# A fused spectral and expert kernel: five output tiles instead of four, and a build-time plan that counts them

## The chip, the cores and the metric

The kernel runs on one core of a Trainium2 chip, where nothing else runs. The metric is the device time of one execution in microseconds (us). The kernel before took 427.27 us (median of 3 runs, 426.96 to 428.14). One execution of each kernel was also recorded by the profiler, and the traces shown here are of those. In them DVE is VectorE, ACT ScalarE, PE TensorE's matmuls, PEld its weight loads, POOL GpSimd, SP SyncE; L with a number is a line of that kernel's source, so the same statement has different numbers in different kernels.

## The reference, cut to what matters

```python
# x: (8, 2496, 256) float32
X = rfft(x, axis=1);  Y = softshrink(X @ (w_r + i w_i) + (b_r + i b_i), 0.01)
y = irfft(Y, axis=1)                                  # (8, 2496, 256)
e = argmax(mean(y, axis=1) @ w_gate)                  # one of 8 experts per batch row
out = softmax_gate * (relu(y @ w1[e]) @ w2[e])        # w1[e] 256x1024, w2[e] 1024x256
```

The kernel does the transforms as matmuls in fp16 and works on two batch rows at a time: while one row ("batch" below) is in its expert stage, the next is in its transforms. Batches are counted from 0; those with a transposition are 1 to 6. A batch in the steady part takes some 50 us.

## The kernel before

The order of instructions on every engine comes from a list scheduler in the kernel itself. It runs when the kernel is built and takes, one after the other, the piece of work that can start soonest by its own estimates. A `Tok` stands for a buffer of a ring; a piece that needs one can't be planned before the piece that frees the owner of that place.

```python
    def ready(self, o):
        ...
        for k in o.allocs:
            if k.tag in self.rings: ...
            else:
                h = self.hist.setdefault(k.tag, [])
                prev = h[-k.bufs : len(h) - k.bufs + 1] if len(h) >= k.bufs else []
            for p in prev:
                for r in p.rel:
                    if r.done is None:
                        return None
                    t = max(t, r.done)
        return t
```

Output tiles (`ost`, 128 x 512 float32) come from a pool of four. A result is evicted (copied out of the memory that matmuls write to) into such a tile, and the tile is stored to DRAM. The plan doesn't count these tiles. On the chip the fifth request waits until the store of the first has landed.

```python
    BUFS = {"XT": 2, "hs": 2, "z": 3, "V": 3, "Pt": 2}
    opool = pool("op", 4)
    ...
    # add_turned: last 192 columns of a batch; evicted, transposed 32x32 on VectorE, stored in four pieces
        def ev(eng):
            oc["o"] = ost = opool.tile([P, 2, D], FP32, name="ost")     # tile 10 of the batch
            ...
        e = S.evac(2 * n, ev, v, deps=[m, gb_op])
        def tr(_):
            oc["t"] = ot = opool.tile([P, 2, D], FP32, name="ost")      # tile 11 of the batch
            nc.vector.transpose(out=ot..., in_=oc["o"]...)
        e = S.op("DVE", 0.5, tr, v, deps=[e], lat=0.6)
        ...
        S.op("POOL", 3.0, st, v, deps=[e], dma=1.2)
    ...
    # transforms of the next batch, group q: the sum that a complex product by three matmuls needs
            def sm(_, cell=cell):                                       # L895
                X = cell["X"].rearrange("p h a r i k -> p (h a) r (i k)")
                nc.vector.tensor_add(out=X[:, :, 2], in0=X[:, :, 0], in1=X[:, :, 1])
            so = S.op("DVE", 0.34, sm, vt(f + 0.01), deps=e_ops, lat=0.48)
            ...                                                         # L914: matmuls that read X
```

Of the kernel before, what the change touches and what calls it, by code (L numbers as in the profile page):

```python
# [113 lines left out]
class Ring:  # L114
# [13 lines left out]
    def take(self, k):  # L128
        p = self.first(k)
        for i in range(p, p + k.wide):  # L130
            self.owner[i] = k
        self.at = (p + k.wide) % len(self.owner)
        return p
# [115 lines left out]
def kernel(  # L249
# [21 lines left out]
    def pool(name, bufs, **kw):  # L271
        return ctx.enter_context(tc.tile_pool(name=name, bufs=bufs, **kw))
# [2 lines left out]
    XIN = 5 * XROW + 2 * D  # L275
    XF = 2
    X0_CUTS = ((4, 12), (12, 20), (20, 22))
    BUFS = {"XT": 2, "hs": 2, "z": 3, "V": 3, "Pt": 2}
    cpool = pool("consts", 1)
    xpool = pool("xp", 2)  # L280
    apool = pool("ap", 1)
    bpool = pool("bp", 2)
    ppool = pool("pp", BUFS["Pt"])
    tpool = pool("tp", BUFS["XT"])
    zpool = pool("zp", BUFS["z"])
    Ypool = pool("Yp", BUFS["z"])
    vpool = pool("vp", BUFS["V"])
    v2pool = pool("v2p", 2)
    ypool = pool("yp", 2)
    hpool = pool("hp", BUFS["hs"])  # L290
    wpool = pool("wp", 2)
    gpool = pool("gp", 2)
    opool = pool("op", 4)
    spool = pool("sp", 1)
    dpool = pool("dp", 2, space=bass.MemoryType.DRAM)
    psum = pool("ps", 1, space=bass.MemoryType.PSUM)
# [88 lines left out]
    S = Schedule(BANKS)  # L385
# [14 lines left out]
    def bank(tag):  # L400
        return ps[:, BASE[tag] + S.bank[tag]]
# [53 lines left out]
    for i in range(WARM):  # L455
        def dummy(_):
            nc.tensor.matmul(pw, warm[:, 0:P], warm)
        o = S.op("PE", 0.43 if i < COLD else 0.216, dummy, 1e6 + i)
# [18 lines left out]
    c1, c2, c3 = ([S.fixed(t)] for t in X0_AT[1:])  # L477
# [736 lines left out]
    def add_fast(b, c, ns, nl, cell, h_ops, hk, wk, tt, gb_op, v0):  # L1214
        (t0, t1_, t2, t3), t_tok = tt
        th, m = nl // 2, nl // 4
# [4 lines left out]
        vt = lambda x: v0 + PERIOD * (c * 8 + 8 + x) / 44  # L1221
# [36 lines left out]
        def prod(x, dst, a, bb, start, deps, allocs=(), after=None):  # L1258
            def mm(_):
                if start:  # L1260
                    fc[dst[0]] = bank(tag).rearrange(
                        "p (h i c) -> p h i c", h=2, i=2)
                for t in range(2):
                    for f in range(4):
                        nc.tensor.matmul(  # L1265
                            fc[dst[0]][0:m, dst[1], t, :], A[a](f, t), bb(f),
                            start=start and t == 0 and f == 0,
                            stop=f == 3,
                            skip_group_check=True)
            return S.mm([P] * 8, mm, vt(x), deps=deps, allocs=allocs, after=after)  # L1270

        ost = lambda t, h: fc["o", t][0:m, :, P * h : P * h + P]

        def take(x, t, h, deps):
            def ev(eng):
                if ("o", t) not in fc:
                    fc["o", t] = opool.tile([P, 2, D], FP32, name="ost")
                src = fc["E"][0:m, 0]
                if eng == "ACT":
                    nc.scalar.activation(out=ost(t, h), in_=src, func=AFT.Copy,  # L1280
                                         scale=gbc_t[b][0:m])
                else:
                    nc.vector.tensor_scalar_mul(out=ost(t, h), in0=src,
                                                scalar1=gbc_t[b][0:m])
            return S.evac(256, ev, vt(x), deps=deps)

        def add(x, t, h, half, deps):
            def ad(_):
                nc.vector.scalar_tensor_tensor(  # L1289
                    out=ost(t, h), in0=fc["F"][0:m, half], scalar=gbc_t[b][0:m],  # L1290
                    in1=ost(t, h), op0=ALU.mult, op1=ALU.add)
            return S.op("DVE", 0.36, ad, vt(x), deps=deps, lat=0.5)

        p1 = prod(0, ("E", 0), "11", w2(0, 0), True, h_ops[:4], [ek])
        c1 = take(0.1, 0, 0, [p1, gb_op])
        p2 = prod(1.2, ("F", 0), "12", w2(1, 0), True, h_ops, [fk], p1)
        p5 = prod(2.4, ("F", 1), "S1", T(0), False, [o1, t0], after=p2)
        a11 = add(2.5, 0, 0, 0, [p5, c1])
        p6 = prod(3.6, ("E", 0), "S2", T(1), False, [o2, c1, t1_], after=p5)
        u2 = take(3.7, 0, 1, [p6])  # L1300
        p7 = prod(4.8, ("E", 0), "S3", T(2), False, [o3, u2, t2], after=p6)
        u3 = take(4.9, 1, 1, [p7])
        a22 = add(5.0, 1, 1, 1, [u3, p5, a11])
        p4 = prod(6.0, ("E", 0), "22", T(3), False, [u3, t3], after=p7)
        c21 = take(6.1, 1, 0, [p4])
# [8 lines left out]
        for t, deps in ((0, [a11, a12]), (1, [c21, a22])):  # L1314
            def st(_, t=t):
                nc.sync.dma_start(
                    out=out[b, ns + th * t : ns + th * t + th, :].rearrange(
                        "(p i) c -> p i c", i=2),
                    in_=fc["o", t][0:m])
            S.op("SP", 0.3, st, vt(8), deps=deps, dma=0.75)  # L1320

    T_t = {}

    def add_turned(b, ns, nl, s0, cell, h_ops, hk, wk, gb_op, v):

        n = nl - s0
        tag = "o"
        ok = S.tok(tag, BANKS[tag])
        oc = {}
        for h in range(2):  # L1330
            def mm(_, h=h):
                if h == 0:
                    oc["p"] = bank(tag)[:, 0 : 2 * n].rearrange(
                        "p (h t) -> p h t", h=2)
                for ft in range(E):
                    nc.tensor.matmul(  # L1336
                        oc["p"][:, h],
                        w2s_t[b][:, ft].rearrange("p (m h) -> p h m", h=2)[:, h],
                        cell["hs"][:, ft, s0:nl],
                        start=(ft == 0), stop=(ft == E - 1))  # L1340
            m = S.mm([n] * E, mm, v, deps=h_ops, after=m if h else None,
                     allocs=[] if h else [ok])
            hk.rel.append(m)
            wk.rel.append(m)

        def ev(eng):
            oc["o"] = ost = opool.tile([P, 2, D], FP32, name="ost")
            o = ost.rearrange("p h c -> p (h c)")[:, 0 : 2 * n].rearrange(
                "p (h t) -> p h t", h=2)
            if eng == "ACT":  # L1350
                nc.scalar.activation(out=o, in_=oc["p"], func=AFT.Copy,
                                     scale=gbc_t[b])
            else:
                nc.vector.tensor_scalar_mul(out=o, in0=oc["p"],
                                            scalar1=gbc_t[b])
        e = S.evac(2 * n, ev, v, deps=[m, gb_op])
        ok.rel.append(e)

        def tr(_):
            oc["t"] = ot = opool.tile([P, 2, D], FP32, name="ost")  # L1360
            nc.vector.transpose(
                out=ot.rearrange("p h c -> p (h c)")[:, 0 : 2 * n].rearrange(
                    "p (t c h) -> p h t c", h=2, c=32),
                in_=oc["o"].rearrange("p h c -> p (h c)")[:, 0 : 2 * n].rearrange(
                    "p (h t c) -> p h t c", h=2, c=32))
        e = S.op("DVE", 0.5, tr, v, deps=[e], lat=0.6)

        def st(_):
            ot = oc["t"].rearrange("p h c -> p (h c)")[:, 0 : 2 * n]
            ov = out[b, ns + s0 : ns + nl, :].rearrange(  # L1370
                "(t r) (q c) -> q r t c", r=32, q=4)
            for q in range(4):
                nc.gpsimd.dma_start(
                    out=ov[q],
                    in_=ot[32 * q : 32 * q + 32].rearrange(
                        "r (t c) -> r t c", c=64))
        S.op("POOL", 3.0, st, v, deps=[e], dma=1.2)

    def add_moe(b, y_ops, yk, gate):
        w, gb_op, wk = gate  # L1380
# [4 lines left out]
        for c, (ns, nl, tiles) in enumerate(NCH0 if b == 0 else NCH):  # L1385
            x = ns / 64
# [3 lines left out]
            for fc in range(E):  # L1390
                v = v0 + PERIOD * (x + fc * nl / 512) / 44
# [4 lines left out]
                def mm(_, fc=fc, ns=ns, nl=nl, cell=cell, hc=hc, tag=tag):  # L1396
# [5 lines left out]
                    for ch in range(2):  # L1402
# [5 lines left out]
                m = S.mm([nl, nl], mm, v, deps=need + [w], after=m if fc else None,  # L1408
                         allocs=[tk] if fc else [tk, hk])
# [9 lines left out]
                e = S.evac(nl, ev, v, deps=[m])  # L1419
# [7 lines left out]
            for sp, tile_s in enumerate(tiles):  # L1427
                last = b == B - 1 and c == 4 and sp == 1
                if last:
                    tile_s = (256, 2)  # L1430
# [8 lines left out]
                for q in range(4):  # L1439
                    if q // 2 >= tile_s[1]:  # L1440
                        break
                    v = v0 + PERIOD * (x + 6 * nl / 512 + 4 * sp + q) / 44

                    def mm(_, tile_s=tile_s, q=q, cell=cell, oc=oc, tag=tago,
# [8 lines left out]
                        for ft in range(4 * (q % 2), 4 * (q % 2) + 4):  # L1453
# [5 lines left out]
                    m = S.mm([256] * 4, mm, v,  # L1459
                             deps=h_ops[: 4 + 4 * (q % 2)],  # L1460
                             after=m2 if q else None,
                             allocs=[ok] if q == 0 else [ok2]
                             if q == 2 and last else [])
                    m1, m2 = (m if q == 1 else m1 if q else None), m
# [49 lines left out]
                    nc.sync.dma_start(out=out[b, r0 : r0 + P, :],  # L1514
                                      in_=ost[:, 0, :])
                if last:
                    e = S.op("DVE", 0.45, ev_first, v, deps=[m1, gb_op])
                    ok.rel.append(e)
                    e = S.op("ACT", 0.45, ev_last, v, deps=[m2, e])
                    ok2.rel.append(e)  # L1520
                else:
                    e = S.evac(280 * tile_s[1], ev, v, deps=[m2, gb_op])
                    ok.rel.append(e)
                    S.op("SP", 0.5 if b == 0 else 0.3, st, v, deps=[e], dma=0.75)

    for b in range(B):
        if b >= 2:
# [32 lines left out]
```

## Time and profile before

| | before |
|---|---|
| time, us | 427.27 |
| span of the profiled run, us | 425.6 |
| TensorE busy by the profile, us | 412.9 |
| TensorE waits for an instruction of VectorE, 40 us to the end | 2, in all 1.5 us |
| VectorE waits of the transposition for a store | 2, in all 2.0 us |
| lengths of three steady batches, us | 50.24, 49.34, 50.00 |

TensorE is the bound, so only its idle time matters, and the third to sixth rows say what its idle time in the steady part hangs on. The lines behind them are in the prediction.

### The profile page before, as it was taken

Reading aid. Unit: us, or ns where it says so; the run is one execution under the profiler, and the core shown is the slowest. Engines: PE = TensorE matmul, PEld = TensorE weight load, DVE = VectorE, ACT = ScalarE, POOL = GpSimd, SP = SyncE. Lnnn points to the kernel's source line nnn. Section 1 sums busy time; section 2 is a strip of 40 time slices with the busy share of each in tenths; the row PEclk is TensorE's granted clock in tenths of the full one; section 3 lists DMA queues with packets and bytes.
Section 4 is the critical chain, followed back from the end, with each engine's and each line's share of the span. In section 5 each row is a group of like instructions: output and inputs, shape, how many; then the busy total and the mean of one; then the engine's idle time right before and its main releaser. Section 6 shows DMA issues by size and latency. Waiting matters only on the chain.

```text
span 425.6 us, 10587 instructions
## 1 busy us (share of the span) xinstructions
PE 412.9 (97%) x4033; PEld 314.7 (74%) x4033; DVE 344.6 (81%) x682; ACT 350.8 (82%) x719; POOL 60.7 (14%) x104
## 2 busy tenths in 40 slices
PE   6889999999999999999999999999999999999996
PEld 2568777887678867777677877778677787777775
DVE  1697875778799898998989997998979998966561
ACT  3788988888978878897978899888878888888884
POOL 5463100001003020042001220031200030001000
PEclk9999999999999999999999999999999999999999
DMA  7899799629875997779885997859977395432222
GB/s 150 225 181 179 135 274 280 189 85 165 224 239 103 226 241 213 240 149 233 182 238 170 205 242 198 266 131 222 203 209 229 102 188 130 141 112 81 65 100 93
DMA packets 70827, 77.03 MB, mean 181 GB/s; under 512 B 7128, under 2 KB 43696, under 8 KB 70776
## 3 DMA queue, kind: packets, MB, share of 16 engines
q1 hardware_dynamic: 57810, 56.23, 44.7%
q0 software_dynamic: 12704, 19.88, 28.7%
q8 instruction: 31, 0.51, 0.5%
q10 hardware_dynamic: 262, 0.25, 0.2%
q14 instruction: 20, 0.16, 0.1%
HBM read 57.54 MB, written 37.49 MB: 223 GB/s over the span
## 4 chain that ended last, share of the span: by engine, by line
PE 79%; DMA 7%; DVE 6%; ACT 4%; issue 1%; POOL 1%; SPq 0%; DVEq 0%; POOLq 0%
PE ps L1403 27%; PE ps L1265 13%; PE ps L1454 11%; PE ps L914 8%; PE ps L718 4%; DMA out_dram<-ost 3%; PE ps L812 3%; PE ps L547 3%; PE ps L1066 3%; PE ps L876 2%; DMA XB<-fwd 1%; DMA xin<-in_x_dram 1%; ACT hs L1416 1%; PE ps L1336 1%; DMA scr<-V 1%
## 5 line engine op out<-in xcount | busy, mean ns | idle before, releaser
L1416 ACT ACTIVATE hs<-ps 128x512 f16<-128x512 f32 (+3 forms) x320 | 175.9, 574 | 37.5 <-PE ps L1403 34.4
L1403 PE MATMUL ps<-ysb,w1s 128*128 128x512 f16 (+3 forms) x688 | 180.7, 360 | 0.0
L1403 PEld LDWEIGHTS <-w1s 128*128 128x128 f16 x688 | 70.2, 113 | 22.6 <-issue 1.4
L1454 PE MATMUL ps<-w2s,hs 128*128 128x256 f16 x480 | 69.2, 273 | 0.0
L1454 PEld LDWEIGHTS <-hs 128*128 128x128 f16 x480 | 45.8, 98 | 13.9
L1265 PEld LDWEIGHTS <-hs 128*128 128x128 f16 x704 | 46.1, 98 | 13.0
L914 PE MATMUL ps<-w,XT 128*128 128x256 f16 x360 | 50.4, 273 | 1.5 <-DVE XT L895 1.5
L1280 ACT ACTIVATE ost<-ps,gbc 128x256 f32<-128x256 f32 x88 | 42.9, 487 | 2.7 <-PE ps L1265 2.4
L1289 DVE SCALAR_TENSOR_TENSOR ost<-ps,gbc,ost 128x256 f32<-128x256 f32 x66 | 31.2, 479 | 14.8 <-ACT ost L1280 10.4
L914 PEld LDWEIGHTS <-XT 128*128 128x128 f16 x360 | 33.2, 98 | 11.6 <-DVE XT L895 3.8
L1265 PEld LDWEIGHTS <-S 128*128 128x128 f16 x528 | 34.3, 98 | 9.4 <-DVE S L1232 0.8
L938 DVE TENSOR_TENSOR z<-ps,tt 128x512 f16<-128x512 f32 x60 | 39.0, 684 | 1.5
L928 DVE TENSOR_TENSOR tt<-ps,bias 128x1024 f16<-128x1024 f32 x30 | 36.6, 1219 | 4.2 <-PE ps L914 4.0
L1081 ACT CAST ysb<-ps 128x468 f16<-128x468 f32 x63 | 32.8, 578 | 7.6 <-PE ps L1066 7.1
L554 ACT CAST V<-ps 128x512 f16<-128x512 f32 x50 | 29.6, 609 | 2.0 <-PE ps L547 1.8
L822 ACT CAST A<-ps 120x512 f16<-120x512 f32 x47 | 27.7, 605 | 2.8 <-PE ps L812 2.8
L1265 PE MATMUL ps<-T,S 128*128 128x128 f16 x352 | 26.9, 220 | 0.0
L1265 PE MATMUL ps<-T,hs 128*128 128x128 f16 x352 | 26.8, 219 | 0.0
L958 DVE TENSOR_TENSOR Y<-z,cl 64x512 f16<-64x512 f16 x60 | 25.2, 420 | 2.0
L1265 PE MATMUL ps<-w2s,hs 128*128 128x128 f16 x352 | 26.4, 219 | 0.0
L884 ACT CAST XT<-ps 128x512 f16<-128x512 f32 x42 | 24.2, 602 | 0.2
L1066 PE MATMUL ps<-wi,V 120*128 120x117 f16 (+1 forms) x308 | 24.0, 216 | 0.0
(110 smaller groups left out, 619.3 us busy)
## 6 DMA issues: line engine op xcount, KB each, us to landing
out_dram<-ost SPq DMA_DIRECT2D x71, 256.0 KB
scr<-V SPq DMA_DIRECT2D x35, 256.0 KB
xin<-in_x_dram POOLq DMA_DIRECT2D x21, 390.0 KB, 9.6
XB<-fwd SPq DMA_DIRECT2D x30, 256.0 KB
V<-scr SPq DMA_DIRECT2D x14, 504.0 KB
fwd<-A SPq DMA_DIRECT2D x18, 360.0 KB
w1s<-in_moe_w_dram POOLq DMA_DIRECT2D x8, 512.0 KB, 7.6
w2s<-in_moe_w_dram POOLq DMA_DIRECT2D x8, 512.0 KB, 8.9
```

Source lines behind the costliest of these rows:

```text
L554: COPY[eng](out=hc["V"][:, n * u : n * u + n].rearrange("p i c -> p (i c)"), in_=hc["p", u])
L914: nc.tensor.matmul(pm[:, D * a : D * a + D], cell["X"][:, ch, a, t].rearrange("p i k -> p (i k)"), w4[:, ch, t, :], start=(ch == 0), stop= ...
L928: nc.vector.tensor_add(out=cell["tt"], in0=cell["T", 2].rearrange("p (a c) -> p a c", a=2).unsqueeze(1).to_broadcast([P, 2, 2, D]), in1=bi ...
L938: nc.vector.tensor_add(out=cell["z"][:, r], in0=cell["T", 1 - r].rearrange("p (a c) -> p a c", a=2), in1=cell["tt"][:, r])
L1066: nc.tensor.matmul(o, V2[:, g, ch * P : ch * P + P], w)
L1081: COPY[eng](out=yv[:, :, 12 * gb : 12 * gb + 12].rearrange("p a (g j) -> p a g j", j=3), in_=pi[:, 0:468].rearrange("p (g a j) -> p a g j" ...
L1265: nc.tensor.matmul(fc[dst[0]][0:m, dst[1], t, :], A[a](f, t), bb(f), start=start and t == 0 and f == 0, stop=f == 3, skip_group_check=True)
L1280: nc.scalar.activation(out=ost(t, h), in_=src, func=AFT.Copy, scale=gbc_t[b][0:m])
L1289: nc.vector.scalar_tensor_tensor(out=ost(t, h), in0=fc["F"][0:m, half], scalar=gbc_t[b][0:m], in1=ost(t, h), op0=ALU.mult, op1=ALU.add)
L1403: nc.tensor.matmul(ph[:, 0:nl], w1v[:, ch, fc // 4, :, fc % 4], ysb_t[b][:, ch, ns : ns + nl], start=(ch == 0), stop=(ch == 1))
L1416: nc.scalar.activation(out=o, in_=i, func=AFT.Relu)
L1454: nc.tensor.matmul(oc["p"][:, i, :], cell["hs"][:, ft, ts], w2s_t[b][:, ft, :], start=(ft == 0), stop=(ft == E - 1))
```

## The change

The intent: one more output tile, so that an eviction doesn't wait for a store, and a plan that knows when a store frees a tile. Every request of a tile becomes a token of the ring "ost", freed by its store (or, for the tile that is only transposed, by the transposition).

```diff
-    BUFS = {"XT": 2, "hs": 2, "z": 3, "V": 3, "Pt": 2}
+    BUFS = {"XT": 2, "hs": 2, "z": 3, "V": 3, "Pt": 2, "o": 5}
-    opool = pool("op", 4)
+    opool = pool("op", BUFS["o"])
 ... add_turned
-        e = S.evac(2 * n, ev, v, deps=[m, gb_op])
+        okt = [S.tok("ost", BUFS["o"]) for _ in range(2)]
+        e = S.evac(2 * n, ev, v, deps=[m, gb_op], allocs=okt[:1])
-        e = S.op("DVE", 0.5, tr, v, deps=[e], lat=0.6)
+        e = S.op("DVE", 0.5, tr, v, deps=[e], lat=0.6, allocs=okt[1:])
+        okt[0].rel.append(e)
-        S.op("POOL", 3.0, st, v, deps=[e], dma=1.2)
+        okt[1].rel.append(S.op("POOL", 3.0, st, v, deps=[e], dma=1.2))
 ... the same for the two halves of chunks 1 to 3 and for the plain chunks (cut)
```

More of the change, by code (lines that the diff above doesn't have):

```diff
@@ L1272, in add_fast, with take @@
         ost = lambda t, h: fc["o", t][0:m, :, P * h : P * h + P]
-        def take(x, t, h, deps):
+        okt = [S.tok("ost", BUFS["o"]) for _ in range(2)]
+        def take(x, t, h, deps, allocs=()):
             def ev(eng):
@@ L1284, in ev @@
                                                 scalar1=gbc_t[b][0:m])
-            return S.evac(256, ev, vt(x), deps=deps)
+            return S.evac(256, ev, vt(x), deps=deps, allocs=allocs)
         def add(x, t, h, half, deps):
@@ L1294, in add_fast @@
         p1 = prod(0, ("E", 0), "11", w2(0, 0), True, h_ops[:4], [ek])
-        c1 = take(0.1, 0, 0, [p1, gb_op])
+        c1 = take(0.1, 0, 0, [p1, gb_op], [okt[0]])
         p2 = prod(1.2, ("F", 0), "12", w2(1, 0), True, h_ops, [fk], p1)
@@ L1301, in add_fast @@
         p7 = prod(4.8, ("E", 0), "S3", T(2), False, [o3, u2, t2], after=p6)
-        u3 = take(4.9, 1, 1, [p7])
+        u3 = take(4.9, 1, 1, [p7], [okt[1]])
         a22 = add(5.0, 1, 1, 1, [u3, p5, a11])
@@ L1319, in st @@
                     in_=fc["o", t][0:m])
-            S.op("SP", 0.3, st, vt(8), deps=deps, dma=0.75)
+            o = S.op("SP", 0.3, st, vt(8), deps=deps, dma=0.75)
+            okt[t].rel.append(o)
     T_t = {}
@@ L1355, in ev @@
                                             scalar1=gbc_t[b])
-        e = S.evac(2 * n, ev, v, deps=[m, gb_op])
+        okt = [S.tok("ost", BUFS["o"]) for _ in range(2)]
+        e = S.evac(2 * n, ev, v, deps=[m, gb_op], allocs=okt[:1])
         ok.rel.append(e)
@@ L1516, in add_moe @@
                 if last:
-                    e = S.op("DVE", 0.45, ev_first, v, deps=[m1, gb_op])
+                    e = S.op("DVE", 0.45, ev_first, v, deps=[m1, gb_op],
+                             allocs=[S.tok("ost", BUFS["o"])])
                     ok.rel.append(e)
@@ L1521, in add_moe @@
                 else:
-                    e = S.evac(280 * tile_s[1], ev, v, deps=[m2, gb_op])
+                    okt = S.tok("ost", BUFS["o"])
+                    e = S.evac(280 * tile_s[1], ev, v, deps=[m2, gb_op],
+                               allocs=[okt])
                     ok.rel.append(e)
-                    S.op("SP", 0.5 if b == 0 else 0.3, st, v, deps=[e], dma=0.75)
+                    okt.rel.append(S.op("SP", 0.5 if b == 0 else 0.3, st, v,
+                                        deps=[e], dma=0.75))
     for b in range(B):
```

## The prediction

> **What bounds the kernel now.** I read the page first: the busy shares and the 40 slices. TensorE is busy 97% of a span of 425.6 us, and the clock row grants it 9 tenths or more everywhere, so it is not throttled.
>
> ```profile
> PE 412.9 (97%) x4033; PEld 314.7 (74%) x4033; DVE 344.6 (81%) x682; ACT 350.8 (82%) x719; POOL 60.7 (14%) x104
> ```
>
> The reader is to see that only 425.6 - 412.9 = 12.7 us of the span has TensorE idle. The view by stretches puts 6.6 us of that into the first 50 us (10.00 - 6.43, and 40.00 - 36.91) and 3.9 us into the last 25.6 us, where the kernel fills and drains. The 350 us between hold the remaining 2.1 us. A change of output buffers can reach only those 2.1 us, unless it upsets something.
>
> Next I asked where the 2.1 us lie. The list of TensorE's own waits, from 40 us on, has two lines, of which one carries almost all:
>
> ```profile
> PE ps L914 <- DVE XT L895: 1.5, 2, 0.9
> PE ps L876 <- DMA XB<-fwd: 0.6, 1, 0.6
> ```
>
> The columns are total, number of times, longest. Two waits of 0.9 and 0.6 us are for a VectorE addition. To see whether they cost time, I cut the steady part at the same instruction of four following batches (L1403, a piece of the chain that ended last, at 170.78, 221.02, 270.36 and 320.36 us):
>
> ```profile
> 170.78:221.02 50.24, 49.34 (x492) 37.80 (x491) 45.14 (x89) 42.37 (x89) 7.72 (x13) 1.00 0.84 205
> 221.02:270.36 49.34, 49.34 (x492) 37.81 (x491) 45.22 (x89) 42.44 (x89) 7.58 (x13) 1.00 0.85 209
> 270.36:320.36 50.00, 49.37 (x492) 37.80 (x491) 45.16 (x89) 42.48 (x89) 7.55 (x13) 1.00 0.84 206
> ```
>
> The second number is the length, the third TensorE's busy time. All three batches do the same TensorE work, 49.34 to 49.37 us. The middle one has no gap; the first is 50.24 - 49.34 = 0.90 us longer, the third 50.00 - 49.37 = 0.63 us. So the two waits pass one for one into the length of a batch.
>
> What VectorE was doing just then is in its order of time, first around 199 us (batch with the gap), then around 248 us (batch without one):
>
> ```profile
> 197.37 0.69 DVE L884 CAST XT<-ps 128x512 f16<-128x512 f32 x1
> 199.18 0.58 DVE L1361 STREAM_TRANSPOSE ost<-ost 128x384 f32<-128x384 f32 x1 [1.12 <-DMA out_dram<-ost]
> 199.68 0.38 DVE L895 TENSOR_TENSOR XT<-XT 128x512 f16<-128x512 f16 x1
> ```
>
> ```profile
> 247.69 0.69 DVE L884 CAST XT<-ps 128x512 f16<-128x512 f32 x1
> 248.52 0.58 DVE L1361 STREAM_TRANSPOSE ost<-ost 128x384 f32<-128x384 f32 x1
> 249.02 0.38 DVE L895 TENSOR_TENSOR XT<-XT 128x512 f16<-128x512 f16 x1
> ```
>
> In brackets is the idle time before an instruction and what ended it. The transposition of the last output chunk waited 1.12 us for an earlier store; the addition that TensorE needs stands behind it. At 298.51 us the same happens with 0.86 us. The chain of waits shows the whole path: 7.41 us of store, the transposition, the addition, the matmul.
>
> ```profile
> 191.68 7.41 DMA out_dram<-ost
> 199.18 0.06 DVE ost L1361
> 199.68 0.40 DVE XT L895
> 200.12 0.61 PE ps L914 x4
> ```
>
> The page books 3% of the span to this store in its chain (two pieces, 7.41 and 7.15 us). That is not what can be saved: other work ran beside the store until its last microsecond.
>
> **What the Trainium skill says.** First, "Perfetto Trace Analysis", Identifying Performance Opportunities, Optimization Strategy: a gap that repeats on the engine that should be saturated can mean that there are too few buffers for the next tile. The trace agrees: the gap comes at the same instruction, in two of the batches. Second, "TensorE: Matmul & The Clock Gate", the table at its head: VectorE takes its queue in strict order. The trace agrees: the addition's input casts had ended by 198.23 us, yet it started at 199.68, behind the transposition. Third, the same trace page, Per-instruction lifecycle, DMA Instruction — HWDGE: the profiled window of such a store leaves out the movement of the data. The trace agrees: the two stores at 191.68 us occupy SyncE's queue for 1.75 us together, but hold their buffers until 199.1. Fourth, "DMA: Bandwidth & Descriptors", Anatomy of one DMA, gives (for the GpSimd path) 2.0 us plus bytes over 436 GB/s, an estimate of 2.6 us for 256 KB. This case doesn't agree: the store waited for was issued at 193.1 at the latest and landed at 199.1, so 6.0 us or more. The DMA view of 191 to 200 us shows why: the 16 engines are nearly always busy, and a weight load of 512 KB takes 10.4 us to land in the same stretch. The measurement decides.
>
> **The change part by part.** It removes no work and adds none: the same 10587 instructions should appear, give or take semaphore ones. Two things change.
>
> *The fifth buffer.* A batch of this stage takes eleven output tiles, and the transposition takes the last: two for chunk 0, two for each of the chunks 1 to 3, one for the first part of chunk 4, then one for its eviction and one for its transposition. Counting back four tiles from the transposition gives the first half of chunk 3, whose store is issued at 193.1 us, about 5 us before the tile is needed. Counting back five gives the second half of chunk 2, whose store was issued near 182.8 us, 15 us before. So the wait goes. Without it the transposition would start 0.14 us after the cast, as at 248 us (248.52 - 248.38): at 198.06 + 0.14 = 198.20. The addition follows 0.50 us later (198.70), the matmul 0.44 us after that (199.14; both steps from the first fence of VectorE and the chain). TensorE is free from 200.12 - 0.90 = 199.22 on. So the whole 0.90 us goes, with 0.08 us to spare. For the other: the cast ends at 297.65, so 297.79, 298.29, 298.73, against TensorE free at 299.45 - 0.63 = 298.82; the whole 0.63 us goes. Sum 1.53 us. The other four transpositions show no wait for a store, so nothing is to be gained there. The buffer adds 2 x 256 x 4 bytes = 2 KB a partition, and no work.
>
> *The order.* The kernel plans its order at build time from its own estimates; the change lets that plan count output tiles. I printed the plan of the kernel before (its order and margins; no time is taken from it) and asked, for each of its 88 output tiles, when the tile five back would be released. In every case it is planned free before it is needed, by 3.4 us at the closest. So the new condition binds nowhere and should not change a choice. Counted four back, it would bind by 0.03 to 0.11 us at five of the six transpositions, which is where the trace waits. I therefore expect the order to stay as it is, or nearly. The plan frees a store's tile some 4.8 us after issue, less than the trace's 6.0, but 3.4 us of margin covers that.
>
> On the path: -1.53 us from the buffer, 0 from the order, 0 added. 427.27 - 1.53 = 425.74.
>
> **Rivals.** (a) *The order changes after all*, because the planner looks only at a limited number of ready pieces and a tile not yet planned free drops out of that count. Against it speak the margins. If it did, TensorE's gaps could be anywhere, and the time 1 to 3 us either way; the 49.34 us of a gapless batch is a floor for the steady part. (b) *The wait moves.* The matmul has only 0.08 us to spare, and the addition could wait for ScalarE's casts or the next eviction instead. For it: VectorE and ScalarE are busy 81 and 82%. Against: the batch at 248 us is this very order without the wait, and it has no gap. A half-returned gain gives 426.5. (c) *Transfers collide.* The transposed tile's four stores start 1 us sooner, while the weight load runs and the DMA share is 0.84. For it: loads of 7.6 to 10.4 us to land. Against: no TensorE wait for a weight load in the list. It would make 426 to 427. (d) *The wait was a matter of luck*, present in two of six batches in the profiled run, more or fewer in others. The three times before span 426.96 to 428.14, which fits zero to a few such waits; then the gain is 0.7 to 2.5 us.
>
> **Range and chances.** The middle is 425.8, rounded towards (b). Down to 424.8: the timed runs had one wait more than the profile, or the order improves slightly. Up to 427.0: the gain is mostly given back. A change of over 2% is 8.5 us, four times all the TensorE idle time that the steady part has, so faster has 1%. Slower by 2% needs a reordering that breaks the plan; 2%. The rest, 97%, is within 2%.
>
> **What would show it.** In the new profile the wait of the transposition for a store should be gone, and TensorE's wait at L914 with it; all three batches cut as above should be near 49.34 us; TensorE should still be busy about 413 us, in a span near 424.1; the order on every engine should be the same. The prediction is wrong if a TensorE wait stands elsewhere in the steady part, if the order differs widely, or if the runs don't get faster though the waits are gone.

## The result, and the profile after

The changed kernel takes 425.01 us (median of 4 runs, 424.9 to 425.48) against 427.47 us of the kernel before in the same rounds (4 runs). The ratio is 0.9944, 95% interval 0.9926 to 0.9961. Here and below a ratio is the mean time of one kernel's runs over that of the other's in the same rounds, so it is not quite the ratio of the medians quoted. By the ratio the gain is some 2.4 us, and the interval runs from 1.7 to 3.2.

The page's busy line of the changed kernel, whose span is 423.3 us:

```profile
PE 411.4 (97%) x4033; PEld 314.5 (74%) x4033; DVE 344.1 (81%) x682; ACT 350.9 (83%) x719; POOL 60.8 (14%) x104
```

The counts of instructions on all five engines are those of before. Set side by side row for row, the orders of both programs are the same on every engine.

The list of TensorE's waits from 40 us on, which had two lines before, is empty. The transposition's wait for a store is gone from VectorE's list. VectorE in order of time, at the first of the two places (transposition L1365, addition L895):

```profile
197.29 0.69 DVE L884 CAST XT<-ps 128x512 f16<-128x512 f32 x1
197.90 0.57 DVE L1365 STREAM_TRANSPOSE ost<-ost 128x384 f32<-128x384 f32 x1
198.39 0.38 DVE L895 TENSOR_TENSOR XT<-XT 128x512 f16<-128x512 f16 x1
```

The transposition starts 0.61 us after the start of the cast, before the cast's drawn end (start plus drawn length, 197.98). In the kernel before it was 1.81 us.

The three batches cut at the same matmuls as in the prediction (columns: stretch, length, TensorE busy, its weight loads, VectorE, ScalarE, GpSimd, clock, DMA share, GB/s):

```profile
170.69:219.77 49.08, 49.08 (x493) 37.81 (x491) 45.05 (x89) 42.30 (x89) 7.59 (x13) 1.00 0.85 210
219.77:268.92 49.15, 49.15 (x492) 37.80 (x491) 45.12 (x89) 42.46 (x89) 7.57 (x13) 1.00 0.85 210
268.92:317.99 49.07, 49.07 (x493) 37.80 (x491) 45.06 (x89) 42.40 (x89) 7.58 (x13) 1.00 0.87 210
```

The reader is to see that the gain in these three, 1.16 + 0.19 + 0.93 = 2.28 us, is all of the span's gain (425.6 - 423.3 = 2.3), and that it is more than the idle time that the profile drew before. Even the batch that seemed without a gap became 0.19 us shorter.

To find the rest, I set the start of every matmul of one trace against the start of the same matmul in the other (4033 each, in the same order). Between 125 us and the end of the matmuls the distance grows by more than 0.06 us at six places only:

| matmul | batch near 200 us | near 250 us | near 300 us | sum |
|---|---|---|---|---|
| L914, behind the addition | 1.06 | 0.08 | 0.80 | 1.94 |
| L812, 8 us later | 0.10 | 0.11 | 0.12 | 0.33 |

Two things hid here. The first is seen in TensorE's order of time. Kernel before, the matmuls ahead of L914 (eight of 128 columns) and L914; then the same in the changed kernel:

```profile
198.62 0.61 PE L876 MATMUL ps<-tf,XB 128*128 128x128 f16 x8
200.12 0.61 PE L914 MATMUL ps<-w,XT 128*128 128x256 f16 x4 [0.90 <-DVE XT L895]
```

```profile
198.54 0.61 PE L876 MATMUL ps<-tf,XB 128*128 128x128 f16 x8
198.99 0.60 PE L914 MATMUL ps<-w,XT 128*128 128x256 f16 x4
```

Without a wait L914 starts 0.45 us after L876, although L876 is drawn 0.61 us long: the drawn ends overlap the next start by 0.16 us. So a drawn gap of 0.90 us is a wait of 1.06 (200.12 - 198.62 less 0.45, with rounding), and a wait of less than 0.16 us is not drawn at all. The second is the matmul L812 behind four matmuls L1454 (L1459 in the changed kernel), kernel before, then changed:

```profile
207.75 0.60 PE L1454 MATMUL ps<-w2s,hs 128*128 128x256 f16 x4
208.29 0.38 PE L812 MATMUL ps<-xin,wa 117*120 117x512 f16 x1
```

```profile
206.60 0.60 PE L1459 MATMUL ps<-w2s,hs 128*128 128x256 f16 x4
207.04 0.38 PE L812 MATMUL ps<-xin,wa 117*120 117x512 f16 x1
```

0.54 us against 0.44: a wait of 0.10 us, again hidden in a "busy" TensorE. VectorE had been late by 1.20 us since the transposition and TensorE by only 1.06; VectorE's instructions stay late by the same amount for these 8 us. That L812 waits for the bank (a part of the matmuls' result memory) that VectorE's L938 frees fits the times (in the batch near 250 us of before L938 starts at 256.89 and 257.50, L812 at 257.63), but the wait list doesn't name it.

### The profile page after: what moved, and what is told of

Read it like the earlier page. It is cut to its first block, busy times and chain, and to the rows that moved or that the text cites. A ratio compares the mean times of both kernels' runs of the same rounds, so it can differ in the third digit from the quotient of the medians.

```text
span 423.3 us, 10596 instructions
## 1 busy us (share of the span) xinstructions
PE 411.4 (97%) x4033; PEld 314.5 (74%) x4033; DVE 344.1 (81%) x682; ACT 350.9 (83%) x719; POOL 60.8 (14%) x104
## 4 chain that ended last, share of the span: by engine, by line
PE 94%; DMA 2%; DVE 1%; POOL 1%; ACT 0%; issue 0%; SPq 0%; DVEq 0%; ACTq 0%; POOLq 0%
PE ps L1408 32%; PE ps L1265 17%; PE ps L1459 12%; PE ps L914 9%; PE ps L718 4%; PE ps L1066 4%; PE ps L547 4%; PE ps L812 4%; PE ps L876 3%; PE ps L1339 2%; DMA xin<-in_x_dram 1%; PE ps L751 1%; PE ps L754 1%; DMA ysb<-in_w_i_dram 1%; PE ps L630 1%; DVE z L766 1%
## 5 line engine op out<-in xcount | busy, mean ns | idle before, releaser
L1459 PE MATMUL ps<-w2s,hs 128*128 128x256 f16 x480 | 69.1, 272 | 0.0
L1459 PEld LDWEIGHTS <-hs 128*128 128x128 f16 x480 | 45.9, 98 | 13.8
L914 PE MATMUL ps<-w,XT 128*128 128x256 f16 x360 | 50.3, 273 | 0.0
L914 PEld LDWEIGHTS <-XT 128*128 128x128 f16 x360 | 33.4, 98 | 9.6 <-DVE XT L895 1.9
L938 DVE TENSOR_TENSOR z<-ps,tt 128x512 f16<-128x512 f32 x60 | 38.9, 683 | 1.5
```

The lines of the kernel that those rows point to most:

```text
L914: nc.tensor.matmul(pm[:, D * a : D * a + D], cell["X"][:, ch, a, t].rearrange("p i k -> p (i k)"), w4[:, ch, t, :], start=(ch == 0), stop= ...
L938: nc.vector.tensor_add(out=cell["z"][:, r], in0=cell["T", 1 - r].rearrange("p (a c) -> p a c", a=2), in1=cell["tt"][:, r])
L1459: nc.tensor.matmul(oc["p"][:, i, :], cell["hs"][:, ft, ts], w2s_t[b][:, ft, :], start=(ft == 0), stop=(ft == E - 1))
```

## The experiments

Each was run beside the kernel before on the same chip. All gave correct results, and each timed run was in the fast state, but for the single run with three tiles, whose state is unknown.

**The changed kernel again**, as a yardstick.

> The changed kernel once more, beside the others on one chip. Expected 425.0 us, 0.5 to 0.6% below the kernel before. Its steady batches, cut at the same first-layer matmul as before, should again be 49.1 us long.

425.07 us (6 runs, 424.79 to 425.21), ratio to before 0.9946 (0.9925 to 0.9967). As expected. In the same rounds the kernel before ranged from 426.25 to 429.46 us (11 runs): its spread is 3.2 us, the changed kernel's 0.4.

**The fifth buffer without the plan.**

```diff
-    opool = pool("op", 4)
+    opool = pool("op", 5)
```

> The kernel before with the pool of output tiles raised from 4 to 5 and nothing else: the plan knows nothing of it. Theory A (the fifth buffer alone does it; the order on all five engines is the same, row for row, with and without the plan's new conditions): 425.0 us, the same as the changed kernel within 0.2 us. Rival B (the plan's new conditions bring part of the gain): slower than the changed kernel by 0.5 us or more.

425.19 us (424.78 to 425.47), ratio 0.9948 (0.9927 to 0.9969), the changed kernel's within 0.0002. Theory A holds: the fifth buffer alone does it. The new conditions of the plan change no instruction's place.

**The plan without the fifth buffer.** The changed kernel with

```diff
-    BUFS = {..., "Pt": 2, "o": 5}
+    BUFS = {..., "Pt": 2, "o": 4}
```

> The changed kernel with 4 in place of 5: the plan counts output tiles, but there is no fifth. Its plan frees a store's tile some 4.8 us after issue, where the trace had 6.0 or more, and so it leaves the transposition ahead of the addition in batches 2 to 5 and only shifts a few other pieces. Theory A: no gain, 427.3 us give or take 0.7, with the transposition still waiting for a store. Rival B: a gain of 0.5 us or more.

427.92 us (426.75 to 428.35), ratio 1.0012 (0.9989 to 1.0035): no gain. TensorE's waits from 40 us on:

```profile
PE ps L914 <- DVE XT L895: 1.7, 2, 0.9
PE ps L1408 <- ACT hs L1421: 0.2, 1, 0.2
```

The two waits of before are there. The plan takes a tile as free 4.8 us after the store's issue; in this trace the stores that the transpositions near 199, 248 and 298 us wait for took 6.5 to 7.5 us, by the counts of their semaphores. (VectorE's list puts the wait near 199 us down to ScalarE; but the store's semaphore was full only at 198.92, 0.1 us before the transposition.) Counting a resource with too short a time brought nothing here.

**The plan without the fifth buffer, but with a longer landing.** As above, and

```diff
             o = S.op("SP", 0.3, st, vt(8), deps=deps, dma=0.75)
+            o.slack = 4.0          # 2.5 by default
```

> 4 buffers, the plan counts them, and is told that such a store frees its tile 1.5 us later than it thinks (about 6.3 us after issue, near the 6.0 of the trace). The plan then puts the addition and two subtractions, 1.1 us of work, ahead of the transposition. Theory D (VectorE's lost time counts): nearly the whole gain without a fifth buffer, 425.0 to 425.8 us, less or more by what else the new order shifts. Rival (a fifth buffer is needed): 427 us.

425.4 us (4 runs, 424.82 to 425.8), ratio 0.9962 (0.994 to 0.9983). Nearly the whole gain with four tiles: the transposition now stands behind the addition and two subtractions, and neither it nor TensorE waits at these places. The edit changes more than that place: by the counts (VectorE 687 instructions instead of 682, ScalarE 714 instead of 719) the plan also moved pieces between the two engines. So the run shows that a fifth tile isn't needed, not what the transposition's place alone is worth. Whether the 0.0016 in ratio to the yardstick is real, these 4 runs can't say.

**Only the transposition's place.** The kernel before, the transposition emitted after the next VectorE instruction.

```diff
+            if o.hold:                       # the transposition
+                held = (o, e)
+                continue
             o.emit(e)
+            if held is not None and e == "DVE":
+                held[0].emit(held[1])
+                held = None
 # (cut: at the latest it is emitted ahead of the next piece on GpSimd)
```

> The kernel before, 4 buffers, the transposition emitted after the next VectorE instruction instead of ahead of it; all else in the same order. In batches 2 to 5 that next instruction is the addition that TensorE waits for. Theory C (the loss is the addition's place in the queue): the whole gain, 425.0 to 425.3 us. Theory D (VectorE has a backlog after this point, so what counts is its lost time, which the swap only shortens by the 0.3 us that the addition takes from the 1.1 us): the matmul L914 no longer waits, but some 0.8 us of the lateness comes back about 8 us later at the matmul L812, whose bank VectorE frees; in all a gain of 0.3 us for each of two waits, 426.7 us.

426.96 us (6 runs, 426.26 to 427.73) against 427.24, ratio 0.9994 (0.9972 to 1.0017): by the times, no difference is shown. The trace tells C from D. VectorE near 198 us (this kernel's lines are 11 higher: addition L906, transposition L1372):

```profile
197.13 0.69 DVE L895 CAST XT<-ps 128x512 f16<-128x512 f32 x1
198.03 0.42 DVE L906 TENSOR_TENSOR XT<-XT 128x512 f16<-128x512 f16 x1 [0.20 <-ACT XT L895]
198.82 0.58 DVE L1372 STREAM_TRANSPOSE ost<-ost 128x384 f32<-128x384 f32 x1 [0.37 <-DMA out_dram<-ost]
```

The matmul behind the addition gained its 1.06 us, as C and D both say. Then 0.61 us of it went back between 203 and 208 us, at matmuls that wait for VectorE's later work: by the comparison of starts the batch's gain is 0.45 us. C falls, by the times too: it forecast a ratio near 0.995, outside the interval. D had the sizes about right and the place wrong: of the 0.61 us only 0.07 came back at L812, and 0.51 before it, at matmuls of L914 and L547. What counts is VectorE's lost time, and a swap only fills part of it.

**The same swap with five buffers.**

> The changed kernel with the transposition after the next VectorE instruction. If nothing of the wait is left with five buffers, this gains nothing: 425.0 us within 0.3. If the addition's place still costs (the trace shows six weight loads of L914 that wait for it by up to 0.3 us each), it is faster by 0.5 us or more.

425.86 us (4 runs, 425.46 to 425.96), ratio 0.9968 (0.9947 to 0.9988): 0.8 us above the yardstick's median, though in other rounds, and against my expectation. The trace bears it out. No store is waited for here; VectorE loses time in another way:

```profile
197.38 0.69 DVE L895 CAST XT<-ps 128x512 f16<-128x512 f32 x1
198.28 0.42 DVE L906 TENSOR_TENSOR XT<-XT 128x512 f16<-128x512 f16 x1 [0.21 <-ACT XT L895]
198.62 0.57 DVE L1376 STREAM_TRANSPOSE ost<-ost 128x384 f32<-128x384 f32 x1
```

The addition also needs ScalarE's half of the cast, so at the head of the queue it makes VectorE wait. In the plan's order the transposition fills that time. The swap costs VectorE 0.33 us a batch (the first instruction after both starts 1.73 us after the cast instead of 1.40) and TensorE 0.26, in three batches in a row.

**A known delay instead of the wait.** The changed kernel, with

```diff
             oc["t"] = ot = opool.tile([P, 2, D], FP32, name="ost")
+            for _ in range({2: 1, 3: 1, 4: 2, 5: 2}.get(b, 0)):
+                nc.vector.tensor_add(out=ot, in0=bias, in1=bias)
```

> The changed kernel with work of no use ahead of the transposition: one 128x512 addition of some 0.6 us in batches 2 and 3, two of them, some 1.2 us, in batches 4 and 5. The result stays right, as the transposition overwrites it. Theory D: a delay of VectorE here passes to TensorE nearly one for one, though TensorE shows hardly any idle time: about 0.5 us at L914 and L812 together for the single dose, 1.1 us for the double, in all 3.3 us, 428.3 us. Rival (slack of VectorE, busy 81%, absorbs it): under 1 us in all.

429.45 us (4 runs, 429.06 to 429.83), some 4.4 us above the yardstick, more than the 3.3 expected because the useless additions took longer than I had put in. Single dose, then double:

```profile
197.67 0.69 DVE L884 CAST XT<-ps 128x512 f16<-128x512 f32 x1
198.28 0.68 DVE L1366 TENSOR_TENSOR ost<-bias 128x512 f32<-128x512 f32 x1
199.07 0.58 DVE L1367 STREAM_TRANSPOSE ost<-ost 128x384 f32<-128x384 f32 x1
```

```profile
297.32 0.69 DVE L884 CAST XT<-ps 128x512 f16<-128x512 f32 x1
297.93 1.41 DVE L1366 TENSOR_TENSOR ost<-bias 128x512 f32<-128x512 f32 x2
299.44 0.58 DVE L1367 STREAM_TRANSPOSE ost<-ost 128x384 f32<-128x384 f32 x1
```

The transposition starts 1.40 and 2.12 us after the cast's start instead of 0.61: 0.79 and 1.51 us late. TensorE lost 0.75 and 1.47 us. The same reckoning for the kernel before (VectorE's delay from its order of time, TensorE's from the comparison of starts):

| where | VectorE late, us | TensorE late, us |
|---|---|---|
| before, near 250 us | 0.22 | 0.18 |
| with one useless addition, near 200 us | 0.79 | 0.75 |
| before, near 298 us | 0.94 | 0.91 |
| before, near 199 us | 1.20 | 1.16 |
| with two, near 300 us | 1.51 | 1.47 |

All five lie on one line: what VectorE loses at this point, less 0.04 us, is lost to TensorE. The other two doses fit as well: the single one near 250 us made VectorE 0.79 and TensorE 0.74 us late, the double one near 350 us both 1.5 us, there at L914 alone. VectorE, busy 81% over the kernel, has next to no slack here.

**One buffer fewer.** The kernel before with a pool of 3.

> The kernel before with 3 output tiles in the pool. If the count of tiles against the landing of the stores is the cause, a tile less must bring waits at the eviction ahead of the transposition (its tile three back lands at 199.1, it is needed at 196.9) and at the second half of chunk 2, about 2 us each and in every batch: 435 to 452 us. If the count were not the cause, about 427 us.

434.3 us (one run, state unknown), 7 us above the kernel before. The direction is right; the size is just under my range, as not every batch had the waits. VectorE and ScalarE now both wait for stores:

```profile
ACT ost L1351 <- DMA out_dram<-ost: 4.6, 3, 2.1
ACT ost L1280 <- DMA out_dram<-ost: 2.5, 2, 1.9
DVE ost L1361 <- DMA out_dram<-ost: 2.5, 1, 2.5
```

**Why the store is late.** The kernel before, four tiles; in batches 1 to 4 (the expectation says 2 to 5) the two weight loads for the batch after next are issued behind the transposed tile's stores.

```diff
+            if o.hold:                       # weight load of batches 3 to 6
+                held = o
+                continue
             o.emit(e)
+            if held is not None and o.frees: # stores of the transposed tile
+                held.emit("POOL")
+                held = None
```

> The kernel before, 4 buffers, with the two weight loads of 512 KB (for the batch after next, needed some 45 us later) issued in batches 2 to 5 after the transposed tile's stores instead of ahead of them, so that they no longer run beside the store that the transposition waits for; the order on all other engines is the same. Theory E (the store lands late, 6 us after issue, because the weight load shares the 16 transfer engines): the store lands 1 us sooner or more, the waits of the transposition at 199 and 298 us shrink below 0.3 us each, and the time is 425.0 to 425.8 us. Rival F (the store takes that long by itself, or because of the loads of the input): the waits stay near 1 us and the time near 427.3 us.

425.08 us (4 runs, 424.82 to 425.25), ratio 0.9947 (0.9928 to 0.9965): the changed kernel's gain, without a fifth tile. GpSimd's queue of the kernel before near 190 us, then of this one:

```profile
190.47 0.77 POOL L1159 DMA_DIRECT2D w1s<-in_moe_w_dram  x1 [4.45 <-PE ps L1403]
197.21 0.71 POOL L1164 DMA_DIRECT2D w2s<-in_moe_w_dram  x1 [5.97 <-PE ps L1066]
```

```profile
198.76 2.33 POOL L1382 DMA_DIRECT2D out_dram<-ost  x4 [12.05 <-DVE ost L1370]
201.53 0.73 POOL L1167 DMA_DIRECT2D w1s<-in_moe_w_dram  x1 [0.44 <-PE ps L1413]
```

SyncE and VectorE of this kernel at the same place:

```profile
191.59 1.75 SPq L1325 DMA_DIRECT2D out_dram<-ost  x2
197.90 0.57 DVE L1370 STREAM_TRANSPOSE ost<-ost 128x384 f32<-128x384 f32 x1
```

The transposition no longer waits. The semaphore that it waits for names the store: it is the first of the two, issued at 191.68 us before and at 191.59 here. The trace keeps the time of each count of that semaphore (the views don't print them), and the sixteenth is the landing. From issue to landing, us:

| batch | before | weight loads moved |
|---|---|---|
| 1 | 6.39 | 3.91 |
| 2 | 7.41 | 5.34 |
| 3 | 6.43 | 4.56 |
| 4 | 7.15 | 4.84 |
| 5, its load not moved | 5.49 | 5.60 |

Where the loads were moved the store took 1.9 to 2.5 us less; where they weren't, 0.1 more. The first weight load moved by 11 us, the second by 5; which of them counts more was not tried. Batch 5 has no input loads beside the store, batches 1 to 4 have: so by these times the input loads lengthen the store too (6.4 to 7.4 us with both kinds, 5.5 with the weight load alone). No run took them alone away; without the weight load they don't make the transposition wait. The comparison of starts shows the same six places with the same sizes as for the changed kernel (1.06, 0.08, 0.80 at L914; 0.10 to 0.12 at L812). Theory E holds. Of F only a share of the input loads in the store's time is left.

No version beat the changed kernel clearly. Its trace has no wait left at these places, so combining the cures was not tried.

## Why the prediction was right or wrong

**The bound, the place and the cause: right.** The wait of the transposition for a store held up the addition behind it, and with that TensorE. The fifth buffer took the wait away, and nothing took its place.

**The order: right.** The new conditions change no instruction's place; all five orders are the same, and the fifth buffer alone gives the same time.

**The size: the fifth buffer's term was too small.** The text says "Sum 1.53 us"; the trace shows 2.27 us (1.94 + 0.33), and the ratio says 1.7 to 3.2. The measured 425.01 us is inside the range, near its lower end, 0.8 us below the middle. Three parts of that term failed:

- "So the whole 0.90 us goes": the drawn idle time was taken as the wait. It leaves out 0.16 us each time, so L914 lost 1.06 and 0.80 us. That is 0.33 us in all.
- "at 248 us": the batch that I took as one without the wait had one, of 0.22 us. The transposition doesn't start 0.14 us after the cast but 0.08 before its drawn end. TensorE's share was 0.08 us at L914, and "The other four transpositions show no wait for a store" was wrong for this one. So the 49.34 us was no floor either; it is 49.1.
- The second place, L812, was not in the sum at all: 0.33 us in three batches. I looked at the next matmul and not at what VectorE's lateness does afterwards.

**The store: misread, without harm to the sum.** The store that the transposition waits for is not the one issued at 193.1 us but the one at 191.68, 6.4 us before the tile was needed and not "about 5". It took 7.41 us, as the prediction's own chain shows; "6.0 us or more" is only a bound, and three expectations lean on it. (The one at 193.09 landed at 200.67, so not both tiles were held until 199.1. The 1.75 us of SyncE run from the start of the first issue to the end of the second; each is drawn 0.33 us long.) The figure of 2.6 us that it is compared with is for GpSimd's path, and this store is SyncE's. The tile five back was stored at 183.38 us, and in the changed kernel that store landed 6.6 us before the transposition, so the wait goes all the same.

**The rivals.** (a), another order, and (b), a wait that moves, did not come about. (c) had a true core that I put on the wrong side: transfers do collide, but that is what makes the wait, not what eats the gain. I had named the weight load as the reason for the slow store; the experiment shows it. (d), luck, fits: the wait's length depends on a store's landing, and the kernel before spreads by 1.2 to 3.2 us in a set of runs, all kernels without the wait by 1.0 or less. I did not profile those other runs, so that their spread comes from this wait is argued, not shown.

## What to carry to other kernels

When a buffer's release waits for a transfer, ask first what runs beside that transfer: here another tile, a planner told of the longer landing, or loads issued 5 to 11 us later each removed most or all of the same loss, and only the first costs memory. Measure a wait of TensorE by the distance between starts, against a place without the wait, since drawn gaps are too short and small waits have none. An engine busy 81% on average can still have no slack in the stretch that counts: delay it by a known amount there and see what comes through.

## What the Trainium skill lacked or had wrong

- "Perfetto Trace Analysis", Identifying the Most-Contended Engine, says that TensorE's busy time is no measure of the distance to its peak, since matmuls are pipelined; its section Per-instruction lifecycle calls the drawn end of a matmul an estimate. It lacks what this does to idle time, and a size: behind eight 128-column matmuls the drawn gap is short by 0.16 us each time (a wait of 1.06 us is drawn as 0.90), and waits of 0.08 and 0.10 us are not drawn.
- "DMA: Bandwidth & Descriptors", Anatomy of one DMA, gives a fixed part and one by size for GpSimd's path, 2.6 us as an estimate for 256 KB. The page says that DMAs started from different engines interleave on the same 16 DMA engines (Issuing engines are not separate DMA queues), but gives no time for a store issued by SyncE beside another queue's loads: 7.4 us beside input loads and a 512 KB weight load, 5.3 with the weight load moved.
